# Chunked RWKV-7 with a SwiGLU FFN on one core: level-2 keys out of the gram products, work moved from VectorE to ScalarE, six weight slices, and new due numbers for the issue order

## The chip, the cores and the metric

The kernel runs on one NeuronCore of a Trainium2 chip. The metric is the device time of one execution in microseconds, and the time of a kernel is the median over its runs. A profile is one single execution, recorded on the chip, with a time of its own.

## What is computed

Four sequences of eight heads go through a recurrence over 768 tokens with a 40x40 state, and the result goes through a normalized SwiGLU FFN (320 to 1536 to 320). Cut to what matters:

```python
for t in range(S):                                    # S = 768, B = 4, H = 8, D = 40
    y[:, :, t] = einsum('bhd,bhde->bhe', rt, state)
    Sa = einsum('bhde,bhe->bhd', state, at)
    state = state * wt[:, :, None, :] - einsum('bhd,bhe->bhde', Sa, bt) + einsum('bhd,bhe->bhde', vt, kt)

x = y.transpose(0, 2, 1, 3).reshape(B * S, H * D)     # 3072 tokens x 320
xn = x / sqrt(mean(x * x) + 1e-6) * rms_g
g = xn @ w_gate
out = (g * sigmoid(g) * (xn @ w_val)) @ w_out         # 320 -> 1536 -> 320
```

The recurrence's inputs are float32. The three weight matrices reach the chip as float64 and are narrowed to float32 there.

## The kernel before, in words

The tokens are cut into 24 chunks of 32 (`C`). Each chunk goes through three stages, and each pair of chunks (`CG = 2`, 256 rows) through a fourth:

- `front(c)`, L511, prepares a chunk two chunks ahead. It loads w and a (tile `wan`), k and b (`kbn`), v (`VU`), turns them on TensorE (`turned`, L490) and walks through five levels, l = 1, 2, 4, 8, 16. Each level has one group of 32 small matmuls, the gram products of keys `K` and vectors `A` (L549); a predicated copy on VectorE puts them into `LT` (L551), `K` and `A` are scaled by decays for the next level, and each level leaves its keys with the tokens on the partitions in `KN[l]`, the natural keys that `main` needs. For levels 4, 8 and 16 the natural keys come out of the gram products themselves: `Ab` has an identity behind its 32 columns, so the group has 56 columns in place of 16, and ScalarE copies 40 of them to `KN` (L554 to L556). For level 1 they are the loaded `kbn`. For level 2 VectorE multiplies `kbn` by `wn` (L542), a second copy of every odd token's decay that four DMAs a chunk bring in.
- `inverse(c)`, L602, inverts a triangular 32x32 matrix for each sequence and head in 31 steps of two VectorE operations (`tmp`, then `Yi`), after a way over DRAM (`LT` to `sB` to `M`), and back by `sY` to `LT`.
- `main(c)`, L623, is the recurrence proper: the chain `X`, `Xs`, `U`, `up`, the new state `ST`; then the outputs `y` from `Sd`, `rE`, `r2` (r with its halves crossed), the scores `As`, and the natural keys. At its end y is turned, normalized (`sq`, `ss`, `x`), turned again, and multiplied by the norm's weight `gcol` on VectorE into `xg` (L737). `r2` is written once in two chunks, by two VectorE copies (L658, L659), beside ScalarE's copy of `rE`.
- `feed(g)`, L739, is the FFN of a pair of chunks in 12 blocks of 128 columns. A block's weights come as one slice of 480 KB into a tile `wf` (L750; `WB = 5` such tiles, L21), two blocks share one PSUM room, and per block TensorE makes gate and value (`ps<-xg,wf`), ScalarE the Silu (`sg`, L758), VectorE the product (`hT`, L759), and TensorE the down-projection into `po` (L760).

At the start `narrow`, L772, turns the weights into float32 in 24 pieces: raw words into a `wf` tile, integer and floating operations on VectorE and ScalarE that put exponent and mantissa together (L781 to L788), and a store to `sW` in DRAM.

What sets the order: nothing is issued where it is written. Every operation is a `Piece` with an engine, a modelled duration and a due number (the first argument of `tt`, `copy`, `pe`, `dma` and so on). `Plan.issue`, L124, plays the pieces through with these durations and writes down one fixed order for each engine: of the pieces that are ready in its model, the one with the smallest due. On TensorE a few more terms take part (L174 to L191): the FFN's pieces are `paced` by the recurrence and may run `AHEAD` of it, a change between tiled (small) and full matmuls costs `SWITCH` in the model and `STICK` in the choice[...]. On the chip each engine then works through its own order, and semaphores decide the times. So a due number moves an instruction in its engine's order and does nothing else. All of `front`'s, `feed`'s and `inverse`'s DMAs stand in one order too, that of the SP queue, apart from `swapped`'s first chunks.

PSUM for everything but `po` is three pairs of banks. `plan.room()` hands them out; a room is given on when its last reader is done, and the first matmul of the next room on that pair waits for it.

Dummy matmuls `po<-ident` (L812) are put in where the model sees TensorE without work in the first 230 us of its own time[...].

Of the kernel before, what the change touches and what calls it, by code (L numbers as in the profile page):

```python
# [16 lines left out]
P = 128  # L17
# [3 lines left out]
WB = 5  # L21
# [20 lines left out]
class Plan:  # L42
# [7 lines left out]
    SWITCH, STICK = 0.1, 3.0  # L50
    WINDOW, ENOUGH, KEEP = 3.41, 1600, 1300

    LINE, FETCH, STALL = 256, 3.6, 5.0
    LOOK, LOW = 1.0, 1300
    AHEAD, FAR = 2.0, 30.0
# [188 lines left out]
def kernel(  # L244
# [197 lines left out]
    wn_ = Turns(1, [P, NI, D], "wn", whole, fill=1.0)  # L442
# [7 lines left out]
    A_ = Turns(2, [P, NI, C], "A")  # L450
# [60 lines left out]
    def front(c):  # L511
# [4 lines left out]
        wa, kb, wn, z["VU"] = wan.next(), kbn.next(), wn_.next(), VU_.next()  # L516
        for i in range(2):
            tokens(d - T, wa, i, 0, w, tk)
            tokens(d - T, wa, i, 1, a, tk)
            swapped(d - T, kb, i, 0, k, tk)  # L520
            swapped(d - T, kb, i, 1, b, tk)
            swapped(d - T, z["VU"], i, 0, v, tk)

            for x in range(2):
                at = i * 64 + x * C
                dma(d - T + 0.7, wn[at:at + C:2], w[2 * i:2 * i + 2, :, c * C + 1:(c + 1) * C:2, :].rearrange("q h s d -> s (q h) d"))
        ps = turned(d, wa.rearrange("p n o e -> p n (o e)")).rearrange("p n (i x t) -> p n i x t", i=2, x=2)
# [11 lines left out]
        copy(d + 2, K.rearrange("p (n i) x s -> p n i (x s)", n=N), turned(d + 2, kb.rearrange("p n o e -> p n (o e)")).rearrange("p n (i s) -> p n i s", i=2))  # L539
        LT = z["LT"] = LT_.next()  # L540
        z["KN"] = {1: flat(kb).rearrange("p a e -> p (a e)"), 2: KN_[2].next()}
        tt(d + 10.8, z["KN"][2][:, 0:NI * D].rearrange("p (a e) -> p a e", e=D), flat(kb)[:, :, 0:D], wn, MUL)  # L542
        for j, l in enumerate(LEVELS):
# [4 lines left out]
            wide = 16 if l <= 2 else 16 + D  # L548
            pe(due - 14.5, 0.95, [mm(gr[half(i), o, n, 0:wide], K[part(o), 2 * n + i].rearrange("p x s -> p (x s)"),  # L549
                              side(A, l, 1)[part(o), 2 * n + i] if l <= 2 else A[part(o), 2 * n + i, 16:]) for n, i, o in each],  # L550
# [3 lines left out]
            if l > 2:  # L554
                z["KN"][l] = KN_[l].next()
                copy(due + 2, z["KN"][l].rearrange("p (n o e) -> p n o e", n=N, o=2), gr.rearrange("p o n t -> p n o t")[:, :, :, 16:wide])  # L556
# [4 lines left out]
            if G == 1 or l == 1:  # L561
                lr = lambda t: t.rearrange("p n x (g h l) -> p n x h (g l)", h=2, l=l)
                tt(due - 0.8, lr(K1)[:, :, :, 0], lr(K)[:, :, :, 0], t[:, :, None, :, 1].to_broadcast((P, NI, 2, 16)), MUL)
            else:
                for x in range(2):
                    tt(due, side(K1[:, :, x], l, 0), side(K[:, :, x], l, 0), by[1], MUL)
            for x in range(2):
                copy(due, side(K1[:, :, x], l, 1), side(K[:, :, x], l, 1))
            if l == 1 or l == 16:
                A1 = A_.next() if l < 16 else aP_.next()  # L570
                A0 = A[:, :, 0:C]
                ends = [(side(A1, l, 1), side(A1, l, 0), side(A0, l, 1), side(A0, l, 0), by[0])]
            else:
# [3 lines left out]
                if l == 2:  # L577
# [5 lines left out]
            for r1, l1, r0, l0, w_ in ends:  # L583
                tt(due, r1, r0, w_, MUL)
                copy(due + 1.2, l1, l0)
            tt(due - 0.6, Tl[2 * l], t[:, :, :, 0], t[:, :, :, 1], MUL)
# [4 lines left out]
        for i, q in each_iq:  # L591
            for o in range(2):
                dma(due, sB[seq(i, q, o)].rearrange("m (s t) -> s m t", s=C), LT[rows(i, 1 - q), o * N + 4 * q:o * N + 4 * q + 4])
        z["M"] = M = M_.next()
        for m in range(4):
            dma(due + 4.2, M[m * BH:(m + 1) * BH].rearrange("p s t -> p (s t)"), sB)
        z["KN"][32] = KN_[32].next()
        copy(due, z["KN"][32].rearrange("p (n o e) -> p n o e", n=N, o=2),
             turned(due - 5.6, K.rearrange("p (n i) x s -> p n (i x s)", i=2)).rearrange("p n (o e) -> p n o e", o=2)[:, :, :, 0:D])
        z["aP"] = A  # L600

    def inverse(c):  # L602
# [6 lines left out]
        for i in range(C - 1):  # L609
            n, m = i // 4 + 1, C - 1 - i  # L610
            tmp = tmp_.next()[:, 0:n * m].rearrange("p (s t) -> p s t", s=n)
            tt(d + i, tmp, Y[:, 0:n, i:i + 1].to_broadcast((P, n, m)), M[:, i:i + 1, i + 1:].to_broadcast((P, n, m)), MUL)
            tt(d + i + 5.6, Y[:, 0:n, i + 1:], Y[:, 0:n, i + 1:], tmp, SUB)
        sY = sY_.next()
        for m in range(4):
            dma(d + C, sY.rearrange("n (j m t) -> m n j t", m=4, t=C)[m], Y[m * BH:(m + 1) * BH])
        for i, q in each_iq:
            for o in range(2):
                dma(d + C - 3.3, LT[rows(i, 1 - q), o * N + 4 * q:o * N + 4 * q + 4], sY[seq(i, q, o)].rearrange("m (s t) -> s m t", s=C))
# [3 lines left out]
    def main(c):  # L623
# [7 lines left out]
        pe(d - 3.8, 0.6, [mm(X[other(i, n), o, col(n % 4)], LT[own(i, n), o * N + n], VU[own(i, n), n, o, 0:D], False, n % 4 == 3)  # L631
                    for n, i, o in by_q], paced=None)
        Sdec = Sdec_.next()
        tt(d, Sdec, ST.rearrange("p n i d -> p (n i) d")[:, :, 0:D], z["T"][32].to_broadcast((P, NI, D)), MUL)
# [5 lines left out]
        for i, q in each_iq:  # L640
            (copy, dcopy)[q](d + 5, VU[other(i, 4 * q), 4 * q:4 * q + 4, :, 0:D].rearrange("p n o d -> p o n d"),
                             U[other(i, 4 * q), :, 0:4 * D].rearrange("p o (n d) -> p o n d", n=4))
        up = plan.room()
        pe(d + 9.9, M40, [mm(up[part(o), i, col(n)], kn(z, 32, i, n, o), VU[half(i), n, o, 0:D]) for n, i, o in each], paced=None)
# [4 lines left out]
        if c % 2 == 0:  # L649
            tk = slice(c * C, (c + 2) * C)  # L650
            t = rn.next()
            for i in range(2):
                dma(d - T, flat(t)[half(i), :, 0:D], r[2 * i:2 * i + 2, :, tk, :].rearrange("q h s d -> s (q h) d"))
            ps = turned(d + 10, t.rearrange("p n o e -> p n (o e)"), None).rearrange("p n (i t) -> p n i t", i=2)
            R["rE"], R["r2"] = rE_.next(), r2_.next()
            copy(d + 10.2, R["rE"], ps)

            dcopy(d + 6.6, R["r2"][half(0)], ps[half(1), :, 0])  # L658
            dcopy(d + 8.5, R["r2"][half(1)], ps[half(0), :, 1])  # L659
# [185 lines left out]
```

## Time and profile before

| | |
|---|---|
| median of 13 runs | 1265.73 us |
| lowest and highest | 1257.73 and 1279.42 us |
| time of the profiled execution | 1279.42 us |
| its span, first to last instruction | 1277.6 us |
| TensorE clock granted in it, mean | 0.943 |
| TensorE busy | 1142.0 us (89%) |
| VectorE busy | 886.7 us (69%) |
| ScalarE busy | 466.7 us (37%) |
| DMAs that SP issues | 1410 |

The profiled execution is the slowest of the 13. A row of the profile names a line, an engine and an operation, "output <- inputs" by tile names, the shape, the number of instructions, their busy time, the mean of one in ns, and the engine's idle time just before them with what ended it. One matmul in the code is two records[...]. All VectorE operations of `tt`, `ts` and `stt` stand at helper line L324, all ScalarE copies at L348, all matmuls of `mm` at L368, so the tile names tell them apart.

### The profile page before, as it was taken

The page shows a single profiled execution, that of the slowest core. Times are in us where ns is not written, and L with a number is a line of the kernel's source. Part 1 is how long each engine was busy: PE and PEld are TensorE (multiplying, and loading weights), DVE is VectorE, ACT ScalarE, POOL GpSimd, SP SyncE. Part 2 cuts the span into 40 slices and gives each one's busy share as a digit, 9 for nine tenths or more (in the row PEclk, how much of TensorE's full clock was granted, in tenths as well). Part 3 has the DMA queues.
Part 4 walks back from the last instruction along what each step waited for, and adds up shares of the span by engine and source line. Part 5 has one row for each costly group of instructions (what it writes and reads, how often), then busy time and mean ns, then how long its engine had stood idle before and what let it go on. Part 6 is the DMA issues. An engine that isn't in the chain of part 4 may idle for free.

```text
span 1277.6 us, 58318 instructions
## 1 busy us (share of the span) xinstructions
PE 1142.0 (89%) x25626; PEld 928.4 (73%) x25626; DVE 886.7 (69%) x3012; ACT 466.7 (37%) x1060; POOL 46.5 (4%) x118
## 2 busy tenths in 40 slices
PE   7898679999998998999898998988999997999997
PEld 6898667777676776777677776776777776777775
DVE  6778987868668577677578677677677677577310
ACT  3734553334333343333334333333333333331111
POOL 5000000000000000000000000000000000000000
PEclk9999758999899898998999998998999998999999
DMA  7655673544534535535435535535436545333342
GB/s 106 139 151 164 150 184 79 131 97 109 130 84 121 118 91 119 118 93 126 116 79 136 118 87 129 128 68 138 106 87 141 118 96 123 101 87 101 92 143 60
DMA packets 307902, 145.77 MB, mean 114 GB/s; under 512 B 270784, under 2 KB 284608, under 8 KB 307648
## 3 DMA queue, kind: packets, MB, share of 16 engines
q1 hardware_dynamic: 297856, 140.57, 46.3%
q8 instruction: 201, 3.29, 1.1%
q10 hardware_dynamic: 9792, 1.48, 0.8%
q14 instruction: 53, 0.43, 0.1%
HBM read 125.83 MB, written 16.12 MB: 111 GB/s over the span
## 4 chain that ended last, share of the span: by engine, by line
PE 45%; DVE 24%; SPq 12%; DMA 10%; issue 5%; ACT 2%; POOL 0%; DVEq 0%; ACTq 0%
PE ps L368 29%; SPq L365 12%; PE po L368 8%; DVE tmp L324 5%; DVE Yi L324 5%; PE ps L371 5%; DMA M<-sB 4%; PE po L812 4%; DVE As L324 3%; DVE K L324 2%; DVE hT L324 2%; DVE LT L324 2%; DMA sW<-hT 2%; DVE y L324 1%; DMA wf<-sW 1%
## 5 line engine op out<-in xcount | busy, mean ns | idle before, releaser
L368 PE MATMUL ps<-xg,wf 128*128 128x256 f32 (+1 forms) x1728 | 377.4, 405 | 15.6 <-DMA wf<-sW 7.9
L368 PEld LDWEIGHTS ps<-xg,wf 128*128 128x128 f32 (+1 forms) x1728 | 271.4, 196 | 70.8 <-DMA wf<-sW 9.5
L368 PE MATMUL po<-wf,hT 128*128 128x320 f32 x576 | 197.9, 468 | 25.6 <-DVE hT L324 23.6
L324 DVE TENSOR_TENSOR tmp<-Yi,M 128x60 f32<-128x60 f32 (+24 forms) x744 | 156.1, 210 | 43.7 <-DMA M<-sB 23.9
L324 DVE TENSOR_TENSOR Yi<-Yi,tmp 128x60 f32<-128x60 f32 (+24 forms) x744 | 155.7, 209 | 18.2
L344 ACT ACTIVATE sg<-ps 128x256 f32<-128x256 f32 x144 | 55.2, 384 | 269.1 <-PE ps L368 264.8
L368 PEld LDWEIGHTS po<-wf,hT 128*128 128x128 f32 x576 | 101.3, 195 | 71.0 <-DVE hT L324 32.9
L324 DVE TENSOR_TENSOR hT<-ps,sg 128x256 f32<-128x256 f32 x144 | 60.4, 420 | 96.0 <-ACT sg L344 95.7
L348 ACT COPY KN<-ps 128x640 f32<-128x640 f32 x96 | 66.4, 692 | 163.5 <-DVE LT L324 67.9
L368 PEld LDWEIGHTS ps<-Ab,K 40*64 40x64 f32 x4608 | 81.2, 145 | 31.6 <-issue 16.6
L348 ACT COPY K<-K 128x256 f32<-128x256 f32 x240 | 90.7, 414 | 30.7 <-PE ps L368 25.1
L324 DVE TENSOR_TENSOR K<-K,T 128x512 f32<-128x512 f32 (+1 forms) x192 | 93.2, 489 | 9.2 <-ACT K L348 9.0
L368 PE MATMUL ps<-Ab,K 40*64 40x56 f32 x4608 | 91.2, 232 | 8.8 <-ACT K L348 5.4
L812 PE MATMUL po<-ident 128*128 128x128 f32 x698 | 92.1, 290 | 5.9 <-POOL eye L421 5.2
L812 PEld LDWEIGHTS po<-ident 128*128 128x128 f32 x698 | 86.5, 203 | 7.2 <-POOL eye L421 5.2
L324 DVE COPY_PREDICATED LT<-msk,ps 128x256 f32<-128x256 uint32 x120 | 66.1, 551 | 29.2 <-PE ps L368 21.5
L324 DVE TENSOR_TENSOR As<-ps,msi 128x512 f32<-128x512 f32 (+1 forms) x192 | 80.0, 481 | 7.2 <-PE ps L368 7.2
L368 PEld LDWEIGHTS ps<-As,KN 128*40 128x40 f32 x3072 | 67.0, 127 | 24.2 <-DVE hT L324 7.9
L368 PE MATMUL ps<-As,KN 128*40 128x32 f32 x3072 | 73.4, 208 | 8.0 <-DVE hT L324 6.7
L368 PEld LDWEIGHTS ps<-A,K 40*64 40x64 f32 x3072 | 53.8, 144 | 24.8 <-issue 14.7
L324 DVE TENSOR_TENSOR y<-y,ps 128x256 f32<-128x256 f32 x120 | 50.6, 421 | 19.9 <-PE ps L368 17.5
L368 PE MATMUL ps<-A,K 40*64 40x16 f32 x3072 | 58.9, 214 | 5.7 <-ACT K L348 3.4
(106 smaller groups left out, 1310.1 us busy)
## 6 DMA issues: line engine op xcount, KB each, us to landing
wf<-sW SPq DMA_DIRECT2D x144, 480.0 KB, 4.3
M<-sB SPq DMA_DIRECT2D x96, 128.0 KB, 2.8
sW<-hT SPq DMA_DIRECT2D x24, 240.0 KB, 3.5
wan<-in_w_dram SPq DMA_DIRECT2D x48, 80.0 KB, 3.4
wan<-in_a_dram SPq DMA_DIRECT2D x48, 80.0 KB, 3.5
wn<-in_w_dram SPq DMA_DIRECT2D x96, 40.0 KB, 3.3
rn<-in_r_dram SPq DMA_DIRECT2D x24, 160.0 KB, 6.2
wf<-in_moe_w_out_dram SPq DMA_DIRECT2D x12, 320.0 KB, 3.4
```

The lines of the kernel that those rows point to most:

```text
L324: plan.add("DVE", due, time + 0.00104 * size(o), lambda at: fn(at(o), *m(at)), [o], aps(*args))
L344: plan.add("ACT", due, 0.08 + 0.00083 * size(o), lambda at: nc.scalar.activation(at(o), at(a), f, **kw), [o] + aps(acc), [a])
L348: plan.add("ACT", due, 0.08 + 0.00083 * size(o), lambda at: nc.scalar.copy(at(o), at(a)), [o], [a])
L365: plan.add(by, due, 0.45, lambda at: queue.dma_start(out=o, in_=i), [o], [i], lane=max(0.4, n * 4 / 220e3), since=since)
L368: return o, lhsT, rhs, lambda at: nc.tensor.matmul(at(o), lhsT, rhs, start=start, stop=stop, skip_group_check=True), 4
L371: return o, i, ident, lambda at: nc.tensor.transpose(at(o), i, ident), 2
L812: plan.warm = lambda: nc.tensor.matmul(po_[:, 0, DM:DM + P], ident, ident, start=False, stop=False, skip_group_check=True)
```

## The change

1. Level 2 gets its natural keys as levels 4 to 16 do. Its gram group grows from 16 to 56 columns, ScalarE copies the keys from PSUM, and `wn` with its four DMAs a chunk and VectorE's product go. Level 1 now leads into an `Ab` tile and does the reordering that level 2 did, so `A` needs one tile in place of two.
2. The norm's weight is applied by three ScalarE operations a chunk, with the weight as a per-partition scale, in place of one VectorE product.
3. The two copies of `r2` go to ScalarE.
4. `narrow`: the implicit one of the mantissa is set by a bitwise or in the same VectorE operation that masks it, and the scale of 2^-20 goes into the last product. ScalarE's pass over the mantissa goes.
5. `WB` is 6 in place of 5.
6. Due numbers are changed nearly everywhere, and three constants of the model's choice: `SWITCH`, `STALL`, `AHEAD`.

```diff
-WB = 5
+WB = 6
...
-    SWITCH, STICK = 0.1, 3.0
+    SWITCH, STICK = 0.16, 3.0
...
-    LINE, FETCH, STALL = 256, 3.6, 5.0
+    LINE, FETCH, STALL = 256, 3.6, 8.0
...
-    AHEAD, FAR = 2.0, 30.0
+    AHEAD, FAR = 8.0, 30.0
...
-    wn_ = Turns(1, [P, NI, D], "wn", whole, fill=1.0)
...
-    A_ = Turns(2, [P, NI, C], "A")
+    A_ = Turns(1, [P, NI, C], "A")
...
-            for x in range(2):
-                at = i * 64 + x * C
-                dma(d - T + 0.7, wn[at:at + C:2], w[2 * i:2 * i + 2, :, c * C + 1:(c + 1) * C:2, :].rearrange("q h s d -> s (q h) d"))
...
-        z["KN"] = {1: flat(kb).rearrange("p a e -> p (a e)"), 2: KN_[2].next()}
-        tt(d + 10.8, z["KN"][2][:, 0:NI * D].rearrange("p (a e) -> p a e", e=D), flat(kb)[:, :, 0:D], wn, MUL)
+        z["KN"] = {1: flat(kb).rearrange("p a e -> p (a e)")}
...
-            wide = 16 if l <= 2 else 16 + D
+            wide = 16 if l == 1 else 16 + D
...
-            if l > 2:
+            if l > 1:
                 z["KN"][l] = KN_[l].next()
-                copy(due + 2, z["KN"][l].rearrange("p (n o e) -> p n o e", n=N, o=2), gr.rearrange("p o n t -> p n o t")[:, :, :, 16:wide])
+                copy(due + 9, z["KN"][l].rearrange("p (n o e) -> p n o e", n=N, o=2), gr.rearrange("p o n t -> p n o t")[:, :, :, 16:wide])
...
-            if l == 1 or l == 16:
-                A1 = A_.next() if l < 16 else aP_.next()
+            if l == 16:
+                A1 = aP_.next()
...
-            tt(d + i, tmp, Y[:, 0:n, i:i + 1].to_broadcast((P, n, m)), M[:, i:i + 1, i + 1:].to_broadcast((P, n, m)), MUL)
-            tt(d + i + 5.6, Y[:, 0:n, i + 1:], Y[:, 0:n, i + 1:], tmp, SUB)
+            tt(d + i - 8.8, tmp, Y[:, 0:n, i:i + 1].to_broadcast((P, n, m)), M[:, i:i + 1, i + 1:].to_broadcast((P, n, m)), MUL)
+            tt(d + i + 5.3, Y[:, 0:n, i + 1:], Y[:, 0:n, i + 1:], tmp, SUB)
...
-            copy(d + 10.2, R["rE"], ps)
+            copy(d + 21.1, R["rE"], ps)
-            dcopy(d + 6.6, R["r2"][half(0)], ps[half(1), :, 0])
-            dcopy(d + 8.5, R["r2"][half(1)], ps[half(0), :, 1])
+            copy(d + 6.6, R["r2"][half(0)], ps[half(1), :, 0])
+            copy(d + 8.5, R["r2"][half(1)], ps[half(0), :, 1])
...
-        pe(d + 42.7, 0.6, [mm(xn[half(q), o, m * D:(m + 1) * D],
+        pe(d + 45.3, 0.6, [mm(xn[half(q), o, m * D:(m + 1) * D],
...
-        tt(d + 44.2, xg[c // CG][:, :, c % CG * P:(c % CG + 1) * P], ps, gcol[:, :, None].to_broadcast((P, KT, P)), MUL)
+        for kt in range(KT):
+            scale(d + 37.2, xg[c // CG][:, kt, c % CG * P:(c % CG + 1) * P], ps[:, kt], gcol[:, kt:kt + 1])
...
-                dma(d - 20 + e * per + 7.3, wf, sW[f + e])
+                dma(d - 20 + e * per + 1.6, wf, sW[f + e])
...
-            pe(d, 1.25, [mm(h[e][:, q], wk[e][half(q), 4], x[half(q), 2, :], e == 0, False) for e in range(2) for q in range(2)],
+            pe(d + 0.6, 1.25, [mm(h[e][:, q], wk[e][half(q), 4], x[half(q), 2, :], e == 0, False) for e in range(2) for q in range(2)],
...
-                pe(d + 1 + e * per, 1.75, [mm(h[e][:, q], wk[e][:, 2 * q + kt], x[:, kt, :], False, kt == 1)
+                pe(d + 1 + e * per + 2.2, 1.75, [mm(h[e][:, q], wk[e][:, 2 * q + kt], x[:, kt, :], False, kt == 1)
...
-                act(d + 3 + e * per, sgs[:, e], h[e][:, 0], AF.Silu)
+                act(d + 3 + e * per - 0.2, sgs[:, e], h[e][:, 0], AF.Silu)
                 tt(d + 4 + e * per - 9.8, hTs[:, e], h[e][:, 1], sgs[:, e], MUL)
-                pe(d + (1 + e) * per, 1.1, [mm(po[:, q, 0:DM], hTs[:, e, q * P:(q + 1) * P], wfs[e][:, 5 * P:], f + e == 0, f + e == FT - 1)
+                pe(d + (1 + e) * per + 4.3, 1.1, [mm(po[:, q, 0:DM], hTs[:, e, q * P:(q + 1) * P], wfs[e][:, 5 * P:], f + e == 0, f + e == FT - 1)
...
-        ts(d - 0.9, mt, hi, 0xfffff, None, ALU.bitwise_and)
-        act(d, m, mt, AF.Copy, scale=2.0 ** -20, bias=1.0)
-        stt(d, m, lo.bitcast(U32), 2.0 ** -52, m, MUL, ADD)
-        stt(d + 5, ex, hi, -2147483648, ex, ALU.bitwise_and, ALU.bitwise_or)
-        tt(d, m, m, exf, MUL)
+        ts(d - 0.9, mt, hi, 0xfffff, 0x100000, ALU.bitwise_and, ALU.bitwise_or)
+        stt(d - 1.2, m, lo.bitcast(U32), 2.0 ** -32, mt, MUL, ADD)
+        stt(d + 6.2, ex, hi, -2147483648, ex, ALU.bitwise_and, ALU.bitwise_or)
+        stt(d + 6.7, m, m, 2.0 ** -20, exf, MUL, MUL)
```

The dues left out of this diff move by up to some 12 units in `front`, `inverse` and `main` alike.

## The prediction

> **What bounds the kernel now.** I read the busy table by stage first, then the chain, then TensorE's waits in the middle stage, then what they look like in the timeline, then the SP queue's waits. The stages, as stretches of the span: start, narrowing of the weights, twenty chunks in steady state, end.
>
> ```profile
> core 0: us, PE busy (x) PEld busy (x) DVE busy (x) ACT busy (x) POOL busy (x), PEclk, DMA share, GB/s
> 0.00:117.00 117.00, 102.72 (x1692) 99.29 (x1696) 85.67 (x269) 56.84 (x116) 17.04 (x49) 0.99 0.65 140
> 117.00:218.00 101.00, 76.72 (x1984) 67.23 (x1971) 84.60 (x264) 52.41 (x107) 2.54 (x6) 0.71 0.56 138
> 218.00:1138.00 920.00, 836.62 (x20127) 665.65 (x20128) 666.47 (x2330) 333.50 (x783) 24.53 (x57) 0.96 0.47 110
> 1138.00:1277.00 139.00, 125.93 (x1857) 96.22 (x1852) 49.92 (x150) 23.95 (x54) 2.35 (x6) 0.98 0.36 102
> ```
>
> In the long middle stage TensorE is busy 836.6 of 920 us, VectorE 666.5 (72%), ScalarE 333.5 (36%): TensorE is the bound, with 83 us idle and a clock of 0.96, which is another (1 - 0.96) x 920 = 37 us lost. Only from 117 to 218 is VectorE the fullest (84.6 of 101 us). So work taken from VectorE buys little by itself in the middle; what counts is which waits of TensorE end.
>
> ```profile
> PE 45%; DVE 24%; SPq 12%; DMA 10%; issue 5%; ACT 2%; POOL 0%; DVEq 0%; ACTq 0%
> ```
>
> The chain agrees, and shows SP's queue and the DMAs with 22% as the third party, ScalarE with 2%.
>
> ```profile
> PE po L368 <- DVE hT L324: 21.7, 18, 2.4
> PE ps L368 <- issue: 17.9, 19, 4.4
> PE ps L368 <- DVE hT L324: 12.1, 15, 1.9
> PE ps L368 <- DVE y L324: 9.6, 18, 0.7
> PE ps L368 <- DMA wf<-sW: 7.9, 3, 3.7
> PE ps L368 <- DVE Yi L324: 3.2, 3, 1.4
> PE ps L371 <- ACT KN L348: 2.8, 3, 1.9
> ...
> ```
>
> These are TensorE's waits from 218 to 1190 us: engine and tile, who ended them, total, times, longest. `hT` costs 33.8 us: 21.7 as the down-projection's operand, 12.1 as the last reader of a PSUM room. This is how one looks:
>
> ```profile
> 629.25 1.09 PE L368 MATMUL ps<-Xs,LT 32*32 32x40 f32 x64
> 632.02 1.34 PE L368 MATMUL po<-wf,hT 128*128 128x320 f32 x4 [1.68 <-DVE hT L324]
> 633.20 1.89 PE L368 MATMUL ps<-xg,wf 128*128 128x256 f32 x8
> 635.02 1.12 PE L368 MATMUL ps<-A,K 40*64 40x16 f32 x64
> ```
>
> TensorE stood 1.68 us before a down-projection, with gate and value products and a gram group that needed nothing of it next in its order. It is a matter of order, not of throughput.
>
> ```profile
> SPq L365 <- PE po L368: 173.9, 52, 9.4
> ```
>
> SP stood 173.9 us in 52 waits for a down-projection to free a weight tile, with every later DMA behind it.
>
> [...]
>
> **The change, part by part.** Busy time first. VectorE loses `KN<-kbn,wn` (24 x 824 ns = 19.8 us), the `r` copies (16.5), `xg` (13.3), and gains 48 x 285 - 24 x 422 ns = 3.6 us for level 1's two half-size products in place of one: 46 us less of 887. Narrowing keeps five VectorE operations a piece; the last turns from a product (656 ns) into a scalar-tensor-tensor (655), nothing. ScalarE gains 24 more `KN` copies (x 692 ns = 16.6), 72 scales of 128 elements [...], 24 `r` copies (x 585, the row of `A<-ps` with the same width: 14.0), 4 us for level 1's copies, and loses narrowing's pass (14.4): 48 us more on 467. SP loses 96 issues at 609 ns, 58 us. TensorE: 24 groups of 56 columns in place of 16; 1.16 against 1.12 us in the timeline, 1 us.
>
> Where that and the new order lie on the path, in terms of the sum:
>
> 1. Start, -6 us. Of VectorE's saving, four `KN` products (3.3), four `r` copies (2.8) and two `xg` (1.1), less 0.6, fall before the third chunk, in the stretch that VectorE fills. The new order has 75 more dummy matmuls (416 in place of 341) by then, 75 x 0.24 = 18 us. Between 117 and 218 TensorE is idle 24 us and granted 0.71, worth 29 us more; they fit into that, so I cost them at nothing. Without that cover: +18. Range -15 to +12.
>
> 2. `hT`, -26 us. I laid TensorE's instructions of both built programs out in order, each step with its duration from the timeline (up-projection 1.85, down-projection 1.2, turn 0.95, gram group 1.0 us and so on), and measured the TensorE work between a block's last gate and value product and its down-projection, blocks 10 to 119. What must fit in is the Silu (384 ns), the product (420), and the queues. Before: median 2.5 us, least 0.95, under 2 us in 40 of 110. After: median 6.8, least 3.6, none under 2. From the same layout, the distance from an up-projection room's last matmul to the next user of that pair is under 1.5 us 14 times in 69 before, once after. I take three quarters of 33.8. Range -34 to -12, if VectorE is late by more than the new distance.
>
> 3. `y`, -5 us of 9.6. Work between the last score product and y's turn goes from 2.2 to 7.1 us (median).
>
> 4. Weights and SP, -5 us. From a slice's freeing to its use there lie 25.4 us of TensorE work in place of 21.8: the sixth tile adds a block, the earlier due of the load and the later down-projection take part of it back. With 58 us of issue less, the 7.9 us of TensorE's waits for `wf` should mostly go, and some of those behind `M<-sB`. Range -10 to +3: the loads stand 5.7 due units earlier, so SP may wait before `sB`, `M` and `sY` as before.
>
> 5. ScalarE, +7 us. 48 us of work on an engine that is idle 64% of the middle stage; what shows is where it lengthens a chain or holds a PSUM room. The level-2 room now waits for a 0.69 us copy, the room of the turned x for about 1.1 us in place of 0.55, the room of r for three copies in a row. Eight of the x rooms have only 1.0 us of TensorE work before their next user (also before): 8 x 0.5 = 4 us, and I put 3 for the others. Upper end in the rivals; not below nothing, since no copy leaves ScalarE after the start.
>
> 6. Changes between small and full matmuls go from 472 to 526. A down-projection is 1.34 us in the record after a small group and 1.24 after a full one: up to 54 x 0.1 = 5. I take +3, and +1 for the columns.
>
> 7. Clock, -13 us. Idle of the middle stage becomes 83 - 26 - 5 - 5 + 7 = 54 us; the 37 us lost to half speed scaled with it are 24. Range -25 to +5.
>
> Sum -6 - 26 - 5 - 5 + 7 + 4 - 13 = -44 us. Against the profiled execution, 1279.4 - 44 = 1235. That execution is 13.7 us over the median. I take this excess for clock (the records show no other difference that could vary) and shrink it by 54/83 to 9: about 1226 for the median, 3.1% less. What is late next is TensorE's own work: 837 us of the 920 stay, so the middle can't give more than its idle and its clock.
>
> **The rivals.** *Waits come back elsewhere:* TensorE no longer stands for `hT` but for what comes behind it, a PSUM room, the `sB` to `M` way, the recurrence's own chain. For it: the chain has 22% on SP and DMA, and rooms are three pairs. And some medians of the layout get shorter: `Xs` to v's turn 6.0 to 2.2 us, the rooms of the turned `wan` (2.3 to 1.6) and `kbn` (3.1 to 1.7), x to the next up-projection 12.1 to 5.0. Against: these waits cost TensorE 2 us or less each before, and the steps of `hT`, `y` and the scores have the longer distances. Half of terms 2 to 4 and a quarter of 7: -6 - 18 + 11 - 3 = -16, less some excess: about 1252.
>
> *ScalarE's queue ends last, slower than before:* [...] If three quarters reach the path, 24 x 1.8 = 43 us, against some 25 of remaining gains (terms 1 to 4 with a half of 2, less term 6): 1266 + 18 = 1284. It decides from about 1.0 us a chunk on. Against it: ScalarE is on 2% of the chain, and TensorE's waits for it are a few us.
>
> *It doesn't do what it says:* the order was laid out with modelled times, and the executed program is no looser, because VectorE runs behind the model by more than the new distances. Then only VectorE's saving and the new costs remain, and they cancel: 1264.
>
> **How the numbers follow.** Forecast case (1200 to 1246) 0.62; waits elsewhere (1246 to 1260) 0.18; no looser (within 0.3%, 1262 to 1270) 0.06; ScalarE 0.14. About 0.3% is what a measurement of this kernel can tell from no change. Faster 0.80, same 0.06, slower 0.14. The range of 1195 to 1264 holds the first two cases and the edge of the third.
>
> **What would show it.** Right: `hT` under 10 us among TensorE's waits, clock at 0.965 or more in the middle, TensorE's idle there near 54 us, VectorE 841 and ScalarE 515 us busy in all. Term 1 is wrong if the third chunk begins later than before (222 us), term 4 if SP's wait for `po` is not smaller, term 5 if Silu, `K` or `KN` copies head TensorE's waits. The prediction is wrong as a whole if TensorE's idle stays near 83 us under other names.

## The result, and the profile after

The changed kernel takes 1277.94 us (median of 11 runs, 1270.16 to 1280.19), beside 1266.93 us for the kernel before in the same session (48 runs). The ratio is 1.0092, with a 95% interval of 1.0067 to 1.0117: slower, by 0.9%, where 3.1% faster was forecast.

The profiled execution of the changed kernel took 1279.3 us (span 1277.5), that of the kernel before 1279.42: by chance the same, since the second lies 13.7 us above the median of the 13 runs that it belongs to. So the two profiles show what was exchanged for what, not the 0.9% themselves.

Busy time of the engines first (engine, us, share, instructions), then the chain that ended last:

```profile
PE 1156.0 (90%) x25760; PEld 946.9 (74%) x25760; DVE 838.5 (66%) x2964; ACT 505.8 (40%) x1180; POOL 46.3 (4%) x117
...
PE 41%; DVE 27%; SPq 13%; DMA 9%; issue 4%; ACT 4%; POOL 0%; ACTq 0%; DVEq 0%; POOLq 0%
```

VectorE went from 886.7 to 838.5 us and ScalarE from 466.7 to 505.8: the work moved as the diff says, close to the 841 and 515 of the prediction. The chain has 4 points less of TensorE, 3 more of VectorE and 2 more of ScalarE. The same stages as before:

```profile
core 0: us, PE busy (x) PEld busy (x) DVE busy (x) ACT busy (x) POOL busy (x), PEclk, DMA share, GB/s
0.00:117.00 117.00, 103.75 (x1674) 100.27 (x1675) 85.08 (x277) 57.35 (x117) 16.64 (x48) 0.97 0.65 151
117.00:218.00 101.00, 90.52 (x2338) 78.90 (x2337) 81.91 (x272) 49.41 (x107) 2.47 (x6) 0.92 0.52 131
218.00:1138.00 920.00, 832.10 (x19838) 668.70 (x19839) 621.27 (x2261) 371.15 (x891) 24.83 (x57) 0.95 0.46 105
1138.00:1277.00 139.00, 129.65 (x1913) 99.06 (x1911) 50.21 (x157) 27.90 (x66) 2.35 (x6) 0.99 0.36 102
```

From 117 to 218 us the clock is 0.92 in place of 0.71, and TensorE gets 2338 instructions done in place of 1984. In the long middle stage it is the other way round: 19,838 in place of 20,127, idle 920 - 832.1 = 87.9 us in place of 83.4, clock 0.95 in place of 0.96. In the timeline the third chunk's `main` (its first `ps<-ST,aP`) begins at 211 us in place of 222, but the fourth one's at 246.3 in place of 246.2: the eleven microseconds gained at the start are given back within one chunk. The twenty steps from there to the last `main`, at 1189 in place of 1190, take 943 us in place of 944. An execution of the kernel before at its median is 13.7 us shorter than the profiled one; no profile shows where.

TensorE's waits from 218 to 1190 us (engine and tile, who ended them, total, times, longest):

```profile
PE ps L371 <- ACT x L351: 19.2, 9, 3.5
PE ps L368 <- issue: 17.2, 22, 2.9
PE ps L368 <- DVE hT L324: 10.2, 12, 2.3
PE ps L371 <- DVE tmp L324: 7.4, 4, 3.7
PE ps L371 <- DVE VU L324: 5.7, 9, 1.4
PE ps L371 <- ACT KN L348: 5.5, 4, 1.5
PE ps L368 <- ACT KN L348: 4.0, 6, 2.0
PE ps L371 <- DVE LT L324: 3.8, 1, 3.8
...
```

`hT` has fallen from 33.8 to 10.2 us; the wait of `po` for it and the waits for `wf` and `y` have left the top of the list. The stage is no less idle: other names stand there, `x` first. VectorE's and SP's own waits show two more things that grew (before: 23.9 and 173.9 us):

```profile
DVE tmp L324 <- DMA M<-sB: 69.9, 19, 7.3
...
SPq L365 <- PE po L368: 213.4, 62, 8.2
```

This is how the first of them reaches TensorE. A stretch of the timeline of the changed kernel (start, length, engine, line, operation; in brackets the wait before it):

```profile
667.34 0.20 ACT L344 ACTIVATION_READ_ACCUMULATOR sq<-ps 128x1 f32 x1
...
668.62 1.34 PE L368 MATMUL po<-wf,hT 128*128 128x320 f32 x4
669.36 0.19 DVE L324 TENSOR_TENSOR tmp<-Yi,M 128x31 f32<-128x31 f32 x1 [3.05 <-DMA M<-sB]
...
670.93 0.15 DVE L324 TENSOR_SCALAR ss<-ss 128x1 f32<-128x1 f32 x1
...
671.23 0.85 POOL L354 TENSOR_TENSOR ss<-ss,mhalf 128x1 f32<-128x1 f32 x1 [48.98 <-DVE tmp L324]
...
672.11 0.53 ACT L351 ACTIVATE x<-ps,ss 128x320 f32<-128x320 f32 x1 [3.34 <-POOL ss L354]
...
672.69 0.90 PE L371 MATMUL ps<-ident,x 128*128 128x128 f32 x3 [2.72 <-ACT x L351]
```

VectorE stands 3.05 us at an inverse's first product, whose matrix is still on its way over DRAM. Eight places behind it in VectorE's order is the 0.15 us operation on `ss`: its input `sq` was done at 667.54 us, it began at 670.93. Pool (where the profile names the `tmp` that runs beside it), then ScalarE's `x`, then TensorE wait for that in turn. So TensorE's wait of 2.72 us comes from a queue that the prediction didn't lay out.

### The profile page after: what moved, and what is told of

Same layout as the page of the kernel before. It is cut to its first block, busy times and chain, and to the rows that moved or that the text cites. A ratio compares the mean times of both kernels' runs of the same rounds, so it can differ in the third digit from the quotient of the medians.

```text
span 1277.5 us, 58473 instructions
## 1 busy us (share of the span) xinstructions
PE 1156.0 (90%) x25760; PEld 946.9 (74%) x25760; DVE 838.5 (66%) x2964; ACT 505.8 (40%) x1180; POOL 46.3 (4%) x117
## 4 chain that ended last, share of the span: by engine, by line
PE 41%; DVE 27%; SPq 13%; DMA 9%; issue 4%; ACT 4%; POOL 0%; ACTq 0%; DVEq 0%; POOLq 0%
PE ps L368 28%; SPq L365 13%; DVE tmp L324 7%; DVE Yi L324 7%; PE po L806 5%; DMA M<-sB 5%; PE po L368 5%; PE ps L371 4%; DVE As L324 2%; DVE K L324 2%; DVE LT L324 2%; DVE hT L324 2%; DVE VU L324 2%; DVE y L324 1%; DMA wan<-in_w_dram 1%
## 5 line engine op out<-in xcount | busy, mean ns | idle before, releaser
L368 PE MATMUL ps<-xg,wf 128*128 128x256 f32 (+1 forms) x1728 | 386.2, 413 | 6.0 <-DVE hT L324 4.7
L368 PEld LDWEIGHTS ps<-xg,wf 128*128 128x128 f32 (+1 forms) x1728 | 273.1, 200 | 60.8 <-issue 11.3
L324 DVE TENSOR_TENSOR tmp<-Yi,M 128x60 f32<-128x60 f32 (+24 forms) x744 | 156.4, 210 | 86.5 <-DMA M<-sB 69.9
L368 PE MATMUL po<-wf,hT 128*128 128x320 f32 x576 | 188.5, 451 | 0.6 <-issue 0.6
L348 ACT COPY KN<-ps 128x640 f32<-128x640 f32 x120 | 83.1, 692 | 175.7 <-DVE LT L324 71.0
L368 PEld LDWEIGHTS ps<-Ab,K 40*64 40x64 f32 x6144 | 107.3, 144 | 42.1 <-issue 22.8
L368 PE MATMUL ps<-Ab,K 40*64 40x56 f32 x6144 | 120.6, 231 | 15.6 <-issue 6.9
L368 PEld LDWEIGHTS po<-wf,hT 128*128 128x128 f32 x576 | 103.7, 191 | 30.9 <-issue 1.3
L806 PE MATMUL po<-ident 128*128 128x128 f32 x832 | 107.2, 285 | 5.2 <-POOL eye L421 5.2
L806 PEld LDWEIGHTS po<-ident 128*128 128x128 f32 x832 | 99.7, 197 | 6.8 <-POOL eye L421 5.2
L324 DVE TENSOR_TENSOR As<-ps,msi 128x256 f32<-128x256 f32 x192 | 79.6, 481 | 9.8 <-PE ps L368 9.7
L368 PEld LDWEIGHTS ps<-As,KN 128*40 128x40 f32 x3072 | 65.7, 123 | 24.7 <-issue 14.0
L368 PE MATMUL ps<-As,KN 128*40 128x32 f32 x3072 | 73.5, 204 | 5.0 <-DVE hT L324 2.3
L324 DVE TENSOR_TENSOR T<-T 128x256 f32<-128x256 f32 (+4 forms) x120 | 32.5, 271 | 34.6 <-ACT T L348 33.0
L324 DVE TENSOR_TENSOR y<-ps,T 128x256 f32<-128x256 f32 x24 | 10.2, 423 | 58.5 <-ACT y L348 58.5
```

Of the source, the lines that this page charges most:

```text
L324: plan.add("DVE", due, time + 0.00104 * size(o), lambda at: fn(at(o), *m(at)), [o], aps(*args))
L348: plan.add("ACT", due, 0.08 + 0.00083 * size(o), lambda at: nc.scalar.copy(at(o), at(a)), [o], [a])
L368: return o, lhsT, rhs, lambda at: nc.tensor.matmul(at(o), lhsT, rhs, start=start, stop=stop, skip_group_check=True), 4
L806: plan.warm = lambda: nc.tensor.matmul(po_[:, 0, DM:DM + P], ident, ident, start=False, stop=False, skip_group_check=True)
```

## The experiments

Each of the 18 kernels ran beside the kernel before on the same chip. Ratios to it are compared, not medians, since the kernel before itself had medians from 1262.8 to 1272.9 us beside them. The change has three sorts of parts: the operations (parts 1 to 5), the constants of the model (C: `SWITCH`; `STALL`, a weight in the choice at L193; `AHEAD`), and the dues, in three groups: F, `front`'s with its DMAs; M, the recurrence's in `main` with that of `xg`; R, those of `inverse`, `feed` and `narrow`. Theories at the start: the prediction's own (looser distances, less time, unless ScalarE takes it), against "the new order costs the time". Letters in the expectations: A1, the inverse's products `tmp`, the first of the two operations of a step, stand too early on VectorE (the timeline above); A3, the FFN's new dues; C there, that FFN blocks come bunched between chunk steps.

| operations | order | label | median, us | ratio | 95% |
|---|---|---|---|---|---|
| new | all new (the change) | | 1277.94 | 1.0092 | 1.0067 to 1.0117 |
| new | all old | x1_struct | 1245.82 | 0.985 | 0.9803 to 0.9898 |
| old | all new | x2_order | 1267.21 | 1.0083 | 1.0044 to 1.0122 |
| new | new, inverse's products `tmp` later | x3_tmp | 1277.2 | 1.0123 | 1.0071 to 1.0176 |
| new | new, `feed`'s dues old | x4_feed | 1277.37 | 1.0122 | 1.0068 to 1.0176 |
| new | old, C new | y1_const | 1285.57 | 1.0187 | 1.0144 to 1.023 |
| new | old, M new | y2_main | 1256.95 | 0.9955 | 0.9931 to 0.9978 |
| new | old, F new | y3_front | 1250.44 | 0.9892 | 0.9856 to 0.9928 |
| new | old, R new | y4_rest | 1250.69 | 0.9899 | 0.9856 to 0.9943 |
| new | new, C old | z1_oldconst | 1271.21 | 1.0005 | 0.997 to 1.0039 |
| new | old, `AHEAD` 8 | z2_ahead | 1253.14 | 0.9838 | 0.9776 to 0.9901 |
| new | old, `STALL` 8 | z3_stall | 1273.0 | 1.0024 | 0.9987 to 1.006 |
| new | old, `SWITCH` 0.16 | z4_switch | 1270.67 | 1.0005 | 0.9978 to 1.0033 |
| old | old, C new | b1_const | 1289.53 | 1.0236 | 1.0179 to 1.0293 |
| old | old, `STALL` 8 | b2_stall | 1269.77 | 1.0036 | 1.0007 to 1.0064 |
| old | old, F new | b3_front | 1287.03 | 1.0201 | 1.0144 to 1.0257 |
| old | old, R new | b4_rest | 1245.5 | 0.9868 | 0.9829 to 0.9907 |
| new | F and R new, C and M old | u1_nomain | 1240.91 | 0.9812 | 0.9768 to 0.9856 |
| new, parts 2 and 3 undone | all old | w2_dve | 1245.82 | 0.9831 | 0.979 to 0.9872 |

**Operations or order.** The changed kernel with every old due and constant, and the old operations with every new one:

```diff
 x1_struct, from the changed kernel
-    SWITCH, STICK = 0.16, 3.0
+    SWITCH, STICK = 0.1, 3.0
...
-            tt(d + i - 8.8, tmp, ...
+            tt(d + i, tmp, ...
 x2_order, from the kernel before
-    AHEAD, FAR = 2.0, 30.0
+    AHEAD, FAR = 8.0, 30.0
...
-                pe(d + (1 + e) * per, 1.1, [mm(po...
+                pe(d + (1 + e) * per + 4.3, 1.1, [mm(po...
```

> The changed operations (parts 1 to 5) with the old due numbers and the old three constants. Theory A (the new order costs the time, the operations save it): 1245 to 1258 us, faster than before by 9 to 20, since VectorE has 46 us and SP 58 us less to do and TensorE's order stays as it was. Theory B (ScalarE's 40 us more, PSUM rooms held for its copies): 1272 to 1285, like the changed kernel.

> The old operations and five weight tiles with the new due numbers and constants. Theory A: 1280 to 1300 us, slower than the changed kernel, since the order's loss stands without the operations' gain. Theory B: 1240 to 1260, since the longer distances for hT and y are there and ScalarE has its old work.

The operations with the old order gain 1.5%; the order with the old operations loses 0.8%. So the new operations are no cost, and the loss is one of order: with the new order the kernel is as slow without them (1.0083) as with them (1.0092). `x2_order`, at 1267 us, fell between the ranges of its two theories: taking the operations away did not make the new order slower. The middle stage of `x1_struct`, then its waits from 218 to 1154 us:

```profile
218.00:1138.00 920.00, 843.36 (x20572) 672.80 (x20571) 654.24 (x2365) 385.82 (x915) 25.02 (x59) 0.98 0.46 110
```

```profile
PE ps L368 <- DVE hT L324: 17.3, 17, 5.0
PE ps L368 <- issue: 15.0, 18, 3.1
PE po L368 <- DVE hT L324: 10.8, 15, 1.4
PE ps L368 <- DVE y L324: 7.2, 13, 0.7
...
```

It still waits 28.1 us for `hT`, nearly three times as much as the changed kernel, and is some 2.4% faster: 77 us idle, clock 0.98. A large `hT` wait doesn't make a slow kernel. Beside the changed kernel, idle time differs by 11 us, but the clock's loss, counted as in the prediction, by 28: (1 - 0.98) x 920 = 18 us in place of 46. It is no matter of one profile: the runs of `x1_struct` were granted 0.973 to 0.984 in the mean, those of the changed kernel 0.946 to 0.955. What in the order brings the lower clock isn't shown.

**Two suspects inside the new order.** The inverse's products `tmp` (one in each of its 31 steps) back to their old due, and the seven dues of the FFN back:

```diff
 x3_tmp
-            tt(d + i - 8.8, tmp, ...
+            tt(d + i, tmp, ...
 x4_feed
-                pe(d + 1 + e * per + 2.2, 1.75, ...
+                pe(d + 1 + e * per, 1.75, ...
-                pe(d + (1 + e) * per + 4.3, 1.1, ...
+                pe(d + (1 + e) * per, 1.1, ...
...
```

> The changed kernel with one due number back: the inverse's first product of each step at d + i in place of d + i - 8.8. Theory A1 (the early product stands at the head of VectorE's queue, waits there for M, and the norm's ss, and so x and TensorE, wait behind it): VectorE's wait for M falls from 70 to below 35 us, TensorE's wait for x from 20 to below 6, time 1258 to 1270. Theory A2 (the wait for M only shows slack that would be spent elsewhere): 1274 to 1282, the waits under other names.

> The changed kernel with the FFN's seven due numbers back (loads of the slices later, down-projection earlier). Theory A3 (the later down-projection holds the weight tiles longer, SP stands behind it and M comes late): SP's wait for the down-projection falls from 213 to about 180 us and the time to 1262 to 1270. Theory of the prediction (the longer distance saves the hT waits): hT comes back with 25 to 35 us among TensorE's waits and the time rises to 1285 to 1300.

Neither moves the time beyond its interval (1.0123 and 1.0122). In `x3_tmp` VectorE still waits 62.0 us for `M`, TensorE 17.5 for `x`: the due of these products alone was not what put them ahead of their data, so A1 in this form falls. What the wait for `M` costs isn't tested by it, since the wait stayed. In `x4_feed` the whole of the old waits for `hT` is back (whole span):

```profile
PE po L368 <- DVE hT L324: 25.0, 36, 3.7
PE ps L368 <- ACT x L351: 22.6, 8, 5.4
PE ps L368 <- DVE hT L324: 14.7, 13, 4.2
```

39.7 us of `hT`, where the changed kernel has 11.2 in the whole span and the kernel before 35.7, and the same time. TensorE's idle time in the middle stage is 89 us, as in the changed kernel (88). This is the clearest answer to the prediction's largest term: inside the new order these waits are worth nothing, since other waits shrank by as much. A3 falls with it: SP's wait for `po` rose to 263.5 us where a fall to about 180 was expected.

**Which group of the order.** New operations, old order, one group new:

```diff
 y1_const
-    SWITCH, STICK = 0.1, 3.0
+    SWITCH, STICK = 0.16, 3.0
-    LINE, FETCH, STALL = 256, 3.6, 5.0
+    LINE, FETCH, STALL = 256, 3.6, 8.0
-    AHEAD, FAR = 2.0, 30.0
+    AHEAD, FAR = 8.0, 30.0
 y2_main
-            tt(d + 18, As[:, j, :, i] ...
+            tt(d + 12.9, As[:, j, :, i] ...
...
 y3_front
-            pe(due - 14.5, 0.95, ...
+            pe(due - 15.5, 0.95, ...
...
 y4_rest
-                dma(d - 20 + e * per + 7.3, wf, ...
+                dma(d - 20 + e * per + 1.6, wf, ...
...
```

> The changed operations with the old due numbers, and the three new constants alone. Theory C (AHEAD of 8 in place of 2 lets FFN blocks bunch into every other chunk, and TensorE's order is what costs): 1262 to 1280 us, FFN blocks per chunk interval 5 and 7 in turn. If the loss comes from due numbers of another group: 1240 to 1250, blocks near 6 and 6.

> The changed operations with the old dues, and the recurrence's new dues alone (with those of norm and xg). Theory D (the recurrence's outputs are put later and its VectorE pieces earlier[...]): 1260 to 1280, y's copy and x head the new waits, 50 us or more of VectorE waiting for y. If not: 1240 to 1250.

> The changed operations with the old dues, and the front's new dues alone, its DMAs with them. Theory E (copies of K 11 units earlier and of KN 7 later in ScalarE's queue, loads of w and a 12 and 6 earlier on SP, hold up what the recurrence needs): 1260 to 1280, VectorE's wait for M 55 us or more. If not: 1240 to 1250.

> The changed operations with the old dues, and the new dues of inverse, FFN and narrowing alone. Theory F: the FFN's longer distance helps here, where nothing else is in the way: hT below 12 us among TensorE's waits (30 with the old dues), 1228 to 1240. If the waits come back under other names: 1243 to 1255. If these dues are the ones that cost: 1260 to 1280.

F and R cost nothing that the intervals tell apart from `x1_struct` (0.985), so theory E falls; M costs about 1.1%, C 3.4%. `y1_const` came out above both of its ranges and `y2_main` between its two. What theory D named didn't come in `y2_main`: TensorE waits 0.6 us for `x`, VectorE 38.2 for `M` (32.3 in `x1_struct`). In the traces' middle stages 5 to 7 down-projection blocks, mostly six, lie in a chunk step of `y1_const`; in the changed kernel they mostly alternate 5 and 7, and in the fast `b4_rest` below there are 3 to 9. So bunching is not what makes a kernel slow, and theory C falls. `y4_rest` has only 6.2 us of `hT` and still is no faster than `x1_struct`, as the second of its theories had it. The middle of `y1_const`, and its waits from 218 to 1191 us:

```profile
218.00:1138.00 920.00, 819.55 (x19785) 656.76 (x19788) 632.43 (x2269) 370.89 (x889) 22.77 (x57) 0.96 0.44 105
```

```profile
PE ps L368 <- issue: 26.7, 25, 3.1
PE po L368 <- DVE hT L324: 19.5, 11, 5.6
PE ps L368 <- DVE hT L324: 15.0, 18, 1.6
PE ps L368 <- DVE y L324: 12.6, 21, 1.9
PE ps L371 <- ACT KN L348: 11.2, 7, 4.7
PE ps L371 <- DVE LT L324: 7.3, 6, 2.2
...
```

100 us idle, in place of 77 in `x1_struct`: `hT` has 34.5 of them in two rows, about what it had in the kernel before, "issue" 26.7, and the rest is spread over many names.

**Which constant, and does C explain the change.**

```diff
 z1_oldconst, from the changed kernel: all three constants back
 z2_ahead, from x1_struct
-    AHEAD, FAR = 2.0, 30.0
+    AHEAD, FAR = 8.0, 30.0
 z3_stall, from x1_struct
-    LINE, FETCH, STALL = 256, 3.6, 5.0
+    LINE, FETCH, STALL = 256, 3.6, 8.0
 z4_switch, from x1_struct
-    SWITCH, STICK = 0.1, 3.0
+    SWITCH, STICK = 0.16, 3.0
```

> The changed kernel, all its new dues, with the three constants back. Theory C1 (the constants alone cost some 40 us whatever the dues): 1235 to 1250. Theory C2 (dues and constants were matched to each other, and each set is bad with the other's partner): 1278 or more. The new dues alone, summed from the three groups tried one by one (+11, +5, +5 us on 1246): 1267.

> The changed operations with old dues, and AHEAD of 8 alone. It moves few instructions of TensorE (486 changes of group kind for 484, the same number of down-projections before each chunk within one). If a small change of order moves the time little: 1243 to 1252. If AHEAD is the cause: 1270 or more.

> The changed operations with old dues, and STALL of 8 alone. Like AHEAD it moves few instructions (480 changes for 484): 1243 to 1252. If the order is so sensitive that any reshuffle costs, 1255 or more here and with AHEAD alike.

> The changed operations with old dues, and SWITCH of 0.16 in place of 0.1 alone. The order of the start and the middle differs from the old one as much as with all three constants (406 dummy matmuls as with the three, 479 with none; 466 changes of group kind). Theory S (this constant is the one): 1270 to 1288. Otherwise 1243 to 1255, and the three cost only together.

`AHEAD` does nothing, `STALL` costs 1.7% and `SWITCH` 1.6%. With all dues new, C costs only 0.9% (1.0005 to 1.0092): the groups don't add up, each of them makes a new order out of the whole. `z1_oldconst` bears out neither C1 nor C2; its ratio is near that of the sum, 1267 us. The middle of `z3_stall`:

```profile
218.00:1138.00 920.00, 829.89 (x20057) 661.98 (x20056) 637.72 (x2302) 376.80 (x896) 24.39 (x57) 0.97 0.46 107
```

13.5 us more idle than in `x1_struct`, and 28 us of clock in place of 18. Yet laid out as for the prediction, its TensorE order has the same distances: 2.5 us (median) from up-projection to down-projection and 2.2 to y's turn in both, 480 changes between small and full matmuls against 484. What the prediction measured in the order doesn't tell a kernel 1.7% slower from the other.

**The same groups on the old operations.** The edits are those above, made in the kernel before.

```diff
 b1_const, b2_stall: as y1_const and z3_stall
 b3_front, b4_rest: as y3_front and y4_rest
```

> The old operations and old dues, with the three new constants alone; the pair to y1_const, which was at 1.019 of before. Theory G (the operations gain 1.5% whatever the order): 1.034 of before, near 1305 us. Theory H (the gain of 1.5% belongs to one lucky order; the operations are worth nothing on average): 1.00 to 1.02.

> The old operations and old dues, with STALL of 8 alone; the pair to z3_stall, at 1.002. Theory G: 1.017. Theory H: 1.00 or below.

> The old operations with the front's new dues alone; the pair to y3_front, at 0.989. Theory G: 1.004. Theory H: 0.985 to 0.995.

> The old operations with the new dues of inverse, FFN and narrowing alone; the pair to y4_rest, at 0.990. Theory G: 1.005. Theory H: 0.985 to 0.995.

C costs 2.4% here too, `STALL` alone 0.4% and not 1.7%; F costs 2.0% here and nothing with the new operations; R gains 1.3% here and nothing there. Theory G holds for none of the four; H fits `b4_rest`, nearly `b2_stall` and `b1_const`, and fails for F, which came out above both. The middle of `b4_rest`:

```profile
218.00:1138.00 920.00, 855.74 (x20676) 686.57 (x20674) 679.72 (x2409) 342.57 (x798) 26.02 (x59) 0.97 0.50 114
```

In it `hT` is 6.9 us in the whole span in place of 35.7 (no wait of `po` for it is left), and idle in the middle 64 in place of 83, though the 83 come from an execution 13.7 us above its median. This is what the prediction described, and it comes without any of the new operations: 17 us, by the dues of R alone. Whether the FFN's dues in R do it, or those of the inverse or of narrowing, wasn't tried apart.

Pairing each order with old and new operations gives 1 to 0.985 (old order), 1.0236 to 1.0187 (C), 1.0036 to 1.0024 (`STALL`), 1.0201 to 0.9892 (F), 0.9868 to 0.9899 (R), 1.0083 to 1.0092 (all new). The operations are worth 0.8% on average over these six, between 3.1% gained and 0.3% lost: the order decides how much.

**Without the two groups that cost, and without ScalarE's extra work.**

```diff
 u1_nomain, from the changed kernel: C and M back
-    LINE, FETCH, STALL = 256, 3.6, 8.0
+    LINE, FETCH, STALL = 256, 3.6, 5.0
...
-            tt(d + 12.9, As[:, j, :, i] ...
+            tt(d + 18, As[:, j, :, i] ...
...
 w2_dve, from x1_struct: parts 2 and 3 undone
-            copy(d + 6.6, R["r2"][half(0)], ...
+            dcopy(d + 6.6, R["r2"][half(0)], ...
-        for kt in range(KT):
-            scale(d + 44.2, xg[c // CG][:, kt, ...
+        tt(d + 44.2, xg[c // CG][...], ps, gcol[...], MUL)
...
```

> The changed kernel with the three constants and the recurrence's dues (norm and xg with them) put back; the new dues of front, inverse, FFN and narrowing stay. Theory J (in the full change the loss comes from the constants and from the recurrence's dues, which bring TensorE's waits for x, tmp and VU): 0.985 to 0.992 of before, TensorE's wait for x below 6 us and hT below 10. If front, inverse and FFN dues are what goes wrong together: 1.00 or more.

> The changed operations with the old order, but the norm's weight and the two copies of r2 on VectorE as before (parts 2 and 3 undone); the pair to x1_struct at 0.985. If the gain of x1 comes from VectorE's 30 us less there: 0.992 to 1.00. If it comes from part 1 and the sixth tile, or ScalarE's load costs as much as VectorE's saves: 0.98 to 0.988.

`u1_nomain` has the lowest ratio, 1.9% under the kernel before and, by the two ratios, 2.8% under the changed one; its interval overlaps with those of `x1_struct`, `z2_ahead` and `w2_dve`. It is faster than theory J had it. Its middle stage, its waits from 218 to 1155 us, and VectorE's and SP's:

```profile
218.00:1138.00 920.00, 851.59 (x20765) 682.68 (x20766) 652.00 (x2360) 387.62 (x922) 24.13 (x59) 0.98 0.47 110
```

```profile
PE ps L368 <- issue: 28.0, 28, 2.6
PE ps L368 <- DVE y L324: 12.0, 21, 1.5
PE ps L368 <- DVE hT L324: 6.2, 7, 1.6
PE ps L371 <- ACT VU L348: 4.4, 4, 1.4
...
```

```profile
DVE tmp L324 <- DMA M<-sB: 24.5, 14, 3.4
...
SPq L365 <- PE po L368: 235.7, 62, 11.3
```

Here `hT` has nearly gone and the place stays empty: 68 us idle, clock 0.98, no wait for `x` from 218 to 1190 us, and VectorE waits 24.5 us for `M` in place of 69.9. `w2_dve` stands within the interval of `x1_struct`, with VectorE 872 us busy and ScalarE 475: where those operations run makes no difference that these runs show.

## Why the prediction was wrong, point by point

1. *Start, -6*: right in size: the third chunk begins 11 us earlier, within the range given. But the gain is gone when the fourth begins, and such a gain says little of the whole: with the same operations TensorE gets 2397 instructions done from 117 to 218 us in `x1_struct` and 2240 in `z2_ahead`, which is as fast. That VectorE's saving brings it, as the term said, isn't shown.
2. *`hT`, -26*: the step that failed. The reading of the order was right: with distances of 6.8 us in place of 2.5 the waits went from 33.8 to 10.2 us, almost the three quarters said. Taking the waits' sum for time was wrong: "It is a matter of order, not of throughput" holds for what comes next in the order as well. Idle of the middle stage was 88 us after 83, not 54; 19.2 us of `x`, 7.4 of `tmp`, and more of `VU`, `KN` and `LT` came. `x4_feed` puts all these waits back and takes the same time, `z3_stall` has the distances of `x1_struct` and costs 1.7% more. In `b4_rest` and `u1_nomain`, where nothing else of that size came late, fewer `hT` waits do go with less idle time; in `y4_rest`, which has as few of them, idle is 73 us beside 77 in `x1_struct` and the time no shorter.
3. *`y`, -5*: the wait went (9.6 to under 2 us in the changed kernel), the time did not, as in 2.
4. *Weights and SP, -5*: the waits for `wf` went. But SP's wait for `po`, named as the test, rose to 213.4 us, and is 235.7 in `u1_nomain`. It is 174 to 192 us in the six kernels with the old operations and 207 to 264 in twelve with the new. The new operations come with 96 DMAs fewer to issue and with a sixth weight tile; which of them makes SP stand longer wasn't tried apart. It was no test of the term.
5. *ScalarE, +7*: an upper bound at most. `KN` took 692 ns, the `r` copies 580 (585 estimated) and the scales 371; what was put for the scales was the author's estimate, worked out from no trace. A chunk's three scales fill 0.89 us (at 674.81 us of the changed kernel's trace) where 1.1 were put, and the new copies are 0.692 + 3 x 0.371 + 0.580 = 2.4 us a chunk, three quarters of which are the rival's 1.8. `w2_dve` shows no cost of the scales and the `r` copies. That the sums of busy time came out close is in part luck: level 1's copies brought some 10 us in place of 4, while the scales filled 21.3 us, less than was put, since they overlap (72 x 371 ns are 26.7 us); on VectorE the products `Ab<-A,T` took 386 ns in place of the 285 put for level 1's. The rival that had ScalarE's queue end slower had the right side for the wrong reason: undoing its main suspects changes nothing, and `x1_struct` with all of its copies is 1.5% faster.
6. *Changes between small and full matmuls, +3*: mis-sized, and in the wrong coin. The three constants were priced only by the number of such changes; they cost 0.9% (11 us) within the change, and with the old dues 2.4% on the old operations and 3.4% on the new; `STALL` alone (`z3_stall`) costs 1.7% with no more changes than `x1_struct`. The dues of M, which had no term of their own, cost another 1.9% (`u1_nomain` to `z1_oldconst`).
7. *Clock, -13*: wrong in sign, since it was scaled with an idle time that didn't fall: (1 - 0.95) x 920 = 46 us lost in place of 37. Stretches at half speed are in the trace (a grant of 0.50 from 164.74 to 188.61 us in the kernel before), but that their share follows idle time was the author's estimate, and it doesn't hold. By the middle stages above, idle and clock's loss are 83 and 37 us before, 88 and 46 in the change, 90 and 28 in `z3_stall`, 77 and 18 in `x1_struct`: the clock doesn't follow the sum of the idle time.

The rival *waits come back elsewhere* named the mechanism, also that `x` might come late; it took half of the gain away, where all of it and more went. The sentence "wrong as a whole if TensorE's idle stays near 83 us under other names" is what happened. The layout was made for TensorE alone. VectorE's order, where the operation on `ss` stands behind a product that waits for DRAM (3.05 us in the timeline above), and ScalarE's were in the same built programs and weren't laid out.

What stays open: why the orders that `STALL` 8, `SWITCH` 0.16 and M produce are slow. Shown is that they are, that neither the distances of terms 2 and 3, nor the number of changes, nor bunched blocks, nor the due of the inverse's products `tmp` tells them from faster ones, that the idle time lies under many names, and that part of the loss is idle time and part a lower clock. With the new dues of F and R in place, the waits for `x` and `M` come with M's dues (24.5 us for `M` in `u1_nomain`, 50.7 in `z1_oldconst`, 69.9 in the change); M's dues alone don't bring them (38.2 in `y2_main`). That they are the cost of M is argued, not shown. The sixth weight slice wasn't tried alone.

## What to carry to other kernels

Where a change brings new operations and a new order together, price them apart: the new operations can be tried in the old order, and here they were 1.5% faster where the whole was 0.9% slower. A wait that heads the bound engine's list is worth its time only if nothing else is nearly as late (`x4_feed`, with 39.7 us of `hT`, took the time of the change, which has 11.2); before counting it, lay out the other engines' orders too and look for short operations that stand behind one waiting for a DMA (here 0.15 us behind a wait of 3.05). And a scheduler's constants can cost time though they only shuffle the order: one of them alone moved this kernel by 1.7%, three together by 3.4%.

## What was not expected of the hardware

- ScalarE's copy of 128 x 128 elements took 313 ns (`Ab<-A`, 48 times) in the kernel before, where it belongs to level 2's step, and takes 433 ns in the changed one, where the same row belongs to level 1's step, in runs of one element in place of two. Shape and count are the same. VectorE's product of the same shape in the same step, `Ab<-A,T`, went from 290 to 386 ns. Both go with the operations: `x1_struct`, with the new operations in the old order, has 431 and 392 ns. That the runs make the difference is argued, not measured by itself. The groups of before and of the changed kernel:

```profile
L348 ACT COPY Ab<-A 128x128 f32<-128x128 f32 x48 | 13.2, 313 | 0.6
```

```profile
L348 ACT COPY Ab<-A 128x128 f32<-128x128 f32 x48 | 20.8, 433 | 0.0
```

- TensorE's idle time that the trace puts down to no wait ("issue") is 15 us in the middle of `x1_struct` and 28 us in that of `z3_stall` and of `u1_nomain` (waits of `ps` at L368), with the same operations. It is not what separates slow from fast kernels here, since `u1_nomain` has it too.
